# Bias attention, then a cosine-gated FFN: weight passes, bias load and k loads in other slots

## The chip, the cores and the metric

The kernel runs on one core of a Trainium2 chip. Its time is in microseconds (us) of device time, from one launch to its end; a figure for a kernel is the median of its runs.

## The reference

Attention over 4 batches and 8 heads, 576 positions, head size 64, with an additive bias that a small network computes from the distance of two positions, followed by a feed-forward layer with a cosine gate on the 2304 rows of 512:

```
scores = q @ k.T / 8 + bias[h]          # bias = relu((log1p(|i-j|) / log1p(max(i,1))) * w1 + b1) @ w2
x = softmax(scores) @ v                 # (4, 8, 576, 64), reshaped to (2304, 512)
h = x @ w_in                            # w_in (512, 2048)
out = (h * cos(h)) @ w_out              # w_out (2048, 512)
```

The weights arrive as 64-bit floats and are narrowed on the chip.

## The kernel before

The work is issued by hand, in program order, on every engine. There are three stages.

*Bias* (to about 67 us): TensorE, VectorE, ScalarE and GpSimd compute the bias of all heads, row group by row group, and SP stores each group to memory (`bias_store`, L335). Five query tiles share it: four of 128 queries and one of 64. `load_bias` (L233) reads the bias of a head pair and a tile back into SBUF, for the 64-query tile with two transfers of 64 rows each (L252).

*Attention* (to about 372 us): 16 units (`units`, L71), each a head pair and a batch. A unit has five query tiles; one tile is one *slot* (`slot(i)`, L541), so 80 slots, and slot i belongs to unit i // 5. The third slot of a unit is its tile 2, the fifth is the 64-query tile. In a slot TensorE issues the scores of the slot's tile (`qk`, L383, matmuls at L396, one set for each head, into two score banks `s` used in turn), and VectorE reads a set out with the bias added and the row extremum taken (L409; called the read-out here). ScalarE takes the exponent of the slot before (L427), VectorE its reciprocals (L439, L442), and GpSimd normalises it (L449). TensorE transposes the tile of three slots before (L456, L461); ScalarE and VectorE copy the result out (`keep_main`, `keep_both`, `keep_left`). TensorE multiplies the previous unit's transposed tiles by v (`pv`, L504) and turns the next unit's k and q (`turn`, L220, L195), which ScalarE copies out (L202 to L212). All transposes share three banks (`bank`, L182): each use takes the next in turn and waits for the copy that reads the fourth before it out. After a unit's k is turned, `kswap` (L214) moves its two halves to a second tile kS with two transfers (L216, L217); `qk` multiplies by kN and kS both.

In the same slots the first four chunks of the weights, eight *parts*, are loaded and narrowed into two operands: `load_w` (L76), an absolute value on ScalarE (`abs_w`, L89, L91), four passes of `widen_w` on VectorE (L99, L100, L102, L104; called the passes), a copy on ScalarE (L106) and a subtraction on GpSimd (L108). `W_PLAN` (L537) says in which of ten slots each step of a part stands, counted from slot 0, 10, 20 and so on. In a slot these steps are issued last, behind the copies. `LOAD_PLAN` (L536) says in which slot of a unit SP issues the loads: q of two units on (second slot), k of three units on (first slot), v of the next (fifth slot), four transfers each. GpSimd splits k and q in the slots of `POOL_PLAN` (L527).

SP issues all transfers in program order, and each issue may have to wait (for a buffer, for data, or for an earlier transfer); the ones behind it wait too.

*Feed-forward* (from about 372 us): `ffn1`, gate, `ffn2` in 96 steps, with the other 24 weight parts narrowed in three further groups of steps each (`begin_widen`, L727).

Of the kernel before, what the change touches and what calls it, by code (L numbers as in the profile page):

```python
# [23 lines left out]
def f(ap):  # L24
    return ap.bitcast(F32)
# [3 lines left out]
def kernel(  # L29
# [64 lines left out]
    def widen_w(fc, part, step=None):  # L94
        r, t, b = raw[fc, part], W[fc], wabs[fc, part]
        lo, hi = r[:, :, 0], r[:, :, 1]
        u = b.bitcast(U32)
        if step in (None, 0):
            nc.vector.tensor_scalar(b, b, 2.0**-15, None, ALU.max)  # L99
            nc.vector.tensor_scalar(u, u, 3, 0x3FFFFFF8, ALU.logical_shift_left, ALU.bitwise_and)  # L100
        if step in (None, 1):
            nc.vector.scalar_tensor_tensor(u, lo, 29, u, ALU.logical_shift_right, ALU.bitwise_or)  # L102
        if step in (None, 2):
            nc.vector.scalar_tensor_tensor(u, hi, 0xC0000000, u, ALU.bitwise_and, ALU.bitwise_or)  # L104
        if step in (None, 3):
            nc.scalar.activation(out=t[:, 0, part], in_=b, func=AF.Copy)  # L106
        if step in (None, 4):
            nc.gpsimd.tensor_tensor(t[:, 1, part], b, f(t[:, 0, part]), ALU.subtract)  # L108

    with tc.manual_schedule():  # L110
# [109 lines left out]
        def turn(u, ops):  # L220
            if u >= NU:
                return
            for op in ops:
                if op == "swap":
                    kswap(u)
                elif op[1] == "l":
                    tleft(u, op[0])
                else:
                    tmain(u, op[0], int(op[1]))
# [147 lines left out]
        def alloc_half(u, hf):  # L377
            PT[u, hf] = ptp.tile([128, 2, 4, WQ[hf]], F32, tag=f"h{hf}", name=f"PT{hf}")
            PX[u, hf] = px.tile([128, WQ[hf]], F32, tag=f"x{hf}", name=f"PX{hf}")
# [3 lines left out]
        def qk(u, j, h):  # L383
            t = tiles[j]
            s = ps_s.tile([128, 2, 512], F32, tag="s", name="s")
            if t < 4:
                o = 128 * t + 704 * h
                stats = [(qTs[u % 2][:, o : o + 128], h)]
            else:
                stats = [(qTs[u % 2][:, 512:640], 0), (qTs[u % 2][:, 576:704], 1)]  # L390
            for hf in range(2):
                n = 0
                for a, hh in stats:
                    c0 = HALF * hf + (640 if t == 4 else 576) * hh
                    for kt in (kN, kS):
                        nc.tensor.matmul(  # L396
                            s[:, hf, 0:HALF],
                            a,
                            kt[u][:, c0 : c0 + HALF],
                            start=(n == 0),  # L400
                            stop=(n == 2 * len(stats) - 1),
                        )
                        n += 1
            hp = units[u][0]
            if h == 0:
                P[u, j] = pp.tile([128, 1152], F32, tag="p", name="P")
            neg = P[u, j][:, 576 * h : 576 * h + 576]
            m = sv.tile([128, 2], F32, tag=f"m{h}", name="m")
            nc.vector.tensor_tensor_reduce(  # L409
                neg.rearrange("p (a x) -> p a x", a=2),  # L410
                s[:, :, 0:HALF],
                bias[hp, t, h].rearrange("p (a x) -> p a x", a=2),
                1.0,
                3.0e38,
                ALU.add,
                ALU.min,
                m[:, 0:1],
            )
            cur[u, j, h] = (neg, m)
# [3 lines left out]
        def softmax_exp(u, j, h):  # L423
            neg, m = cur.pop((u, j, h))
            if h == 0:
                dn[u, j] = sv.tile([128, 2], F32, tag="dn", name="dn")
            nc.scalar.activation(  # L427
                out=P[u, j][:, 576 * h : 576 * h + 576],
                in_=neg,
                func=AF.Exp,  # L430
                bias=m[:, 0:1],
                scale=-1.0,
                accum_out=dn[u, j][:, h : h + 1],
            )
# [16 lines left out]
        def ptrans(u, j, h):  # L451
            ps = bank()
            p = P[u, j]
            for c in range(4):
                o = 640 * h + 128 * c
                nc.tensor.transpose(ps[:, 128 * c : 128 * c + 128], p[:, o : o + 128], ident)  # L456
            return ps

        def ptrans_left(u, j):
            ps = bank()  # L460
            nc.tensor.transpose(ps[:, 0:128], P[u, j][:, 512:640], ident)  # L461
            return ps
# [11 lines left out]
        def keep_main(u, j, h, ps):  # L474
            hf, o = where(j)
            (act_copy if h == 0 else dve_copy)(
                PT[u, hf][:, h, :, o : o + 128], ps.rearrange("p (c x) -> p c x", c=4)
            )
# [54 lines left out]
        ]  # L533
        T_EARLY = [["k0", "k1"], ["kl", "swap"], ["q0"], ["ql"], ["q1"]]
        PV_EARLY = [[(-1, 0, (0, 1))], [(-1, 0, (2, 3, 4))], [], [(-1, 1, (0, 1))], [(-1, 1, (2, 3, 4))]]
        LOAD_PLAN = [[(3, "k")], [(2, "q")], [], [], [(1, "v")]]  # L536
        W_PLAN = [("load", 1), ("abs", 5), (0, 6), (1, 6), (2, 7), (3, 9), (4, 9)]  # L537
        get = lambda i: jobs[i] if 0 <= i < len(jobs) else None
        wparts = [(fc, p) for fc in range(WPRE) for p in range(2)]

        def slot(i):  # L541
            u, j = divmod(i, 5)
            now, last, prev = get(i), get(i - 1), get(i - 3)
            heads = lambda x: range(2 if tiles[x[1]] < 4 else 1)
            if now:
                qk(u, j, 0)
            if last:
                softmax_exp(*last, 0)
            if now and tiles[j] < 4:
                qk(u, j, 1)  # L550
            turn(u + 1, T_EARLY[j])
            if last and len(heads(last)) == 2:
                softmax_exp(*last, 1)
            for du, hf, chunks in PV_EARLY[j]:
                if 0 <= u + du < NU:
                    pv(u + du, hf, chunks)
            if i == 1:
                load_bias(0, tiles[-1])
            if prev:
                if prev[1] in (0, 2):  # L560
                    alloc_half(prev[0], prev[1] // 2)
                pt = [ptrans(*prev, h) for h in heads(prev)]
                pl = ptrans_left(*prev)
            if last:
                recip(*last, 0)
                recip(*last, 1)
            if prev:
                if len(pt) == 2:
                    keep_main(*prev, 0, pt[0])
                    keep_main(*prev, 1, pt[1])  # L570
                else:
                    keep_both(prev[0], pt[0])
            if last:
                for h in heads(last):
                    norm(*last, h)
            if prev:
                keep_left(*prev, pl)
            if now:
                for du, x, step in POOL_PLAN[j]:
                    if u + du < NU:  # L580
                        split(u + du, x, step)
                for du, x in LOAD_PLAN[j]:
                    if u + du < NU:
                        load(u + du, x)
                hp, b = units[u]
                if b == B - 1 and hp + 1 < HP:
                    load_bias(hp + 1, tiles[j])
                if u == NU - 1 and j < KD:
                    split_x(0, 0, j)
                for step, at in W_PLAN:  # L590
                    w, r = divmod(i - 0 - at, 10)
                    if r == 0 and 0 <= w < len(wparts):
                        if step == "load":
                            load_w(*wparts[w])
                        elif step == "abs":
                            abs_w(*wparts[w])
                        else:
                            widen_w(*wparts[w], step)
# [113 lines left out]
        loaded, widened, work = 0, 0, []  # L712
# [8 lines left out]
        def widen_step(p, ops):  # L721
            for step in ops:
                widen_w(*p, step)
            if 4 in ops:
                load_next()

        def begin_widen():  # L727
            nonlocal widened
            p = parts[widened]
            W[p[0]] = slots[p[0] % (2 * GF)]  # L730
            abs_w(*p)
            work.extend(lambda s=s: widen_step(p, s) for s in ((0,), (1,), (2, 3, 4)))
            widened += 1

        def ffn_step(i):
# [89 lines left out]
```

## Time and profile before

| | us |
|---|---|
| median of 3 runs (lowest, highest) | 791.92 (790.4, 793.26) |
| profiled execution, its own time | 787.1 |
| its span, first to last instruction | 785.3 |
| TensorE busy in the span | 742.6 |
| VectorE, ScalarE, GpSimd busy | 596.2, 471.2, 407.0 |
| mean granted TensorE clock (share of full) | 0.990 |

The rows further down come from this one execution. A time in front of an instruction is its start from the span's beginning; the second number is its length; in square brackets stand the idle time of its engine before it and what the profile takes for the releaser. PE is TensorE, PEld its weight load, DVE VectorE, ACT ScalarE, POOL GpSimd, SPq the queue in which SP issues transfers. L409 is line 409 of the kernel.

### The profile page before, as it was taken

How to read it: one execution, taken by the hardware profiler on the slowest of the kernel's cores; microseconds unless marked ns; L12 is line 12 of the kernel's file. 1: busy time of each engine (PE TensorE's matmuls, PEld its weight loads, DVE VectorE, ACT ScalarE, POOL GpSimd, SP SyncE). 2: the span in 40 equal slices, each digit the busy share in tenths (PEclk: the TensorE clock that was granted, in tenths of full speed). 3: DMA queues.
4: the chain of work that ended last, by engine and by line, in shares of the span. 5: the costliest groups of instructions: out<-in, count | busy, mean ns of one | idle time of the engine just before them, and what ended most of it. 6: DMA issues, size and time to landing. Idle time of an engine off the chain costs nothing.

```text
span 785.3 us, 13422 instructions
## 1 busy us (share of the span) xinstructions
PE 742.6 (95%) x4602; PEld 604.8 (77%) x4602; DVE 596.2 (76%) x1313; ACT 471.2 (60%) x991; POOL 407.0 (52%) x493
## 2 busy tenths in 40 slices
PE   6888799999999999999899999999999999999997
PEld 2216677777787777776789989988888888898996
DVE  8787477776767677776568878989899898976655
ACT  4997477777777777775355655544454545444332
POOL 2334366767676666658335536455445373544400
PEclk9999699999999999999999999999999999999999
DMA  4787535654673465330010101010111101001112
GB/s 130 237 298 211 128 79 128 173 122 105 133 193 86 119 171 134 70 95 28 1 54 28 54 28 55 27 54 28 54 38 43 54 28 54 1 23 46 53 42 81
DMA packets 70595, 68.45 MB, mean 87 GB/s; under 512 B 30080, under 2 KB 54784, under 8 KB 70528
## 3 DMA queue, kind: packets, MB, share of 16 engines
q1 hardware_dynamic: 70528, 67.60, 31.2%
q8 instruction: 37, 0.61, 0.3%
q14 instruction: 30, 0.25, 0.1%
HBM read 42.00 MB, written 15.61 MB: 73 GB/s over the span
## 4 chain that ended last, share of the span: by engine, by line
PE 83%; DVE 6%; ACT 4%; DMA 3%; issue 3%; POOL 1%; SPq 1%; ACTq 0%; DVEq 0%; POOLq 0%
PE ph L627 25%; PE po L682 24%; PE pv L513 11%; PE s L396 9%; PE pt L456 8%; PE pa L318 3%; PE pt L195 2%; DVE wb L100 1%; ACT rt L334 1%; DMA bt<-sc 1%; DVE P L409 1%; POOL ht L313 1%; PE pt L461 1%; DMA sc<-rt 1%; DVE PT L472 1%
## 5 line engine op out<-in xcount | busy, mean ns | idle before, releaser
L449 POOL TENSOR_SCALAR P<-P,rc 128x576 f32<-128x576 f32 x144 | 109.4, 771 | 90.4 <-DVE rc L442 65.9
L631 ACT ACTIVATE a<-ph,quarter 128x384 int32<-128x384 f32 x96 | 55.8, 581 | 108.0 <-PE ph L627 106.8
L427 ACT ACTIVATE P<-P,m 128x576 f32<-128x576 f32 x144 | 111.0, 771 | 8.6 <-DVE m L409 7.8
L409 DVE CUSTOM_DVE_ANT_0 P<-s,bt 128x576 f32<-128x576 f32 x144 | 103.6, 753 | 14.6 <-DMA vN<-in_v_dram 6.3
L396 PE MATMUL s<-kN,qT 128*128 128x288 f32 x320 | 96.5, 323 | 17.2 <-DVE m L409 17.1
L637 DVE SCALAR_TENSOR_TENSOR r<-a,ph 128x384 f32<-128x384 int32 x96 | 52.9, 551 | 77.9 <-ACT a L631 77.8
L499 POOL TENSOR_TENSOR xs<-xT,xs 128x384 fp32r<-128x384 f32 x96 | 107.2, 1116 | 8.0
L627 PE MATMUL ph<-xs,wpre 128*128 128x384 f32 x576 | 109.4, 338 | 0.8 <-DVE a L646 0.8
L627 PE MATMUL ph<-xs,w 128*128 128x384 f32 x576 | 108.3, 337 | 0.5 <-DVE a L646 0.5
L627 PEld LDWEIGHTS ph<-xs,wpre 128*128 128x128 f32 x576 | 101.8, 188 | 6.3 <-DVE a L646 2.1
L627 PEld LDWEIGHTS ph<-xs,w 128*128 128x128 f32 x576 | 101.3, 188 | 5.5 <-DVE a L646 1.4
L642 ACT ACTIVATE r<-r,hpi 128x384 f32<-128x384 f32 x96 | 59.3, 617 | 69.1 <-DVE r L638 69.1
L396 PE MATMUL s<-kS,qT 128*128 128x288 f32 x320 | 88.4, 297 | 0.1
L456 PEld LDWEIGHTS pt<-ident,P 128*128 128x128 f32 x576 | 63.4, 144 | 29.8 <-issue 8.4
L498 POOL TENSOR_SCALAR xs<-xT 128x384 fp32r<-128x384 f32 x96 | 61.4, 639 | 45.7 <-PE ph L627 45.7
L456 PE MATMUL pt<-ident,P 128*128 128x128 f32 x576 | 81.7, 284 | 2.2 <-POOL P L449 2.2
L472 DVE COPY PT<-pt 128x512 f32<-128x512 f32 x64 | 44.0, 687 | 50.5 <-PE pt L456 50.4
L513 PE MATMUL pv<-PT,vN 128*64 128x320 f32 (+1 forms) x512 | 77.4, 422 | 4.3 <-ACT PT L469 4.1
L396 PEld LDWEIGHTS s<-kN,qT 128*128 128x128 f32 x320 | 60.8, 190 | 21.4 <-DVE m L409 20.1
L682 PE MATMUL po<-w,gh 128*128 128x512 f32 x288 | 75.3, 396 | 0.0
L682 PE MATMUL po<-wpre,gh 128*128 128x512 f32 x288 | 75.2, 396 | 0.0
L656 DVE TENSOR_TENSOR gl<-a,gh 128x384 fp32r<-128x384 f32 x96 | 74.1, 772 | 0.6 <-ACT gh L650 0.6
(88 smaller groups left out, 1343.8 us busy)
## 6 DMA issues: line engine op xcount, KB each, us to landing
sc<-rt SPq DMA_DIRECT2D x36, 295.5 KB
kS<-kN SPq DMA_DIRECT2D x32, 304.0 KB
raw<-in_moe_w_in_dram SPq DMA_DIRECT2D x16, 512.0 KB
raw<-in_moe_w_out_dram SPq DMA_DIRECT2D x16, 512.0 KB
bt<-sc SPq DMA_DIRECT2D x16, 288.0 KB
nk<-in_k_dram SPq DMA_DIRECT2D x32, 128.0 KB
nq<-in_q_dram SPq DMA_DIRECT2D x32, 128.0 KB
vN<-in_v_dram SPq DMA_DIRECT2D x32, 128.0 KB
```

Source lines behind the costliest of these rows:

```text
L396: nc.tensor.matmul(s[:, hf, 0:HALF], a, kt[u][:, c0 : c0 + HALF], start=(n == 0), stop=(n == 2 * len(stats) - 1),)
L409: nc.vector.tensor_tensor_reduce(neg.rearrange("p (a x) -> p a x", a=2), s[:, :, 0:HALF], bias[hp, t, h].rearrange("p (a x) -> p a x", a=2 ...
L427: nc.scalar.activation(out=P[u, j][:, 576 * h : 576 * h + 576], in_=neg, func=AF.Exp, bias=m[:, 0:1], scale=-1.0, accum_out=dn[u, j][:, h ...
L449: nc.gpsimd.tensor_scalar(p, p, r, 1.0, ALU.mult, ALU.mult)
L456: nc.tensor.transpose(ps[:, 128 * c : 128 * c + 128], p[:, o : o + 128], ident)
L498: nc.gpsimd.tensor_scalar(h, src, 1.0, 1.0, ALU.mult, ALU.mult)
L499: nc.gpsimd.tensor_tensor(l, src, f(h), ALU.subtract)
L513: nc.tensor.matmul(ps[64 * h : 64 * h + 64, 0 : WQ[hf]], a, m, start=(c == 0), stop=(c == 4), tile_position=(0, 64 * h), skip_group_check= ...
L627: nc.tensor.matmul(ps, a, x, start=(i == 0), stop=(i == 3 * KD - 1))
L642: nc.scalar.activation(out=r, in_=r, func=AF.Sin, scale=SIN_SCALE, bias=hpi)
L656: nc.vector.tensor_tensor(gl, a, f(G[key][0]), ALU.subtract)
L682: nc.tensor.matmul(O[n][i], a[:, 128 * i : 128 * i + 128], w, start=(i0 == 0 and p == 0), stop=(i0 == GF - 1 and p == 2),)
```

## The change

The first of VectorE's two passes of step 0 keeps its number, the second becomes step 0.5. `W_PLAN` becomes a table by slot, with a table of its own for the first part (`W_FIRST`), and may reach into the ten slots before. Parts 1 to 7 get: load three slots before their ten, abs in their first slot, the passes L99, L100, L102 in the slots of index 2, 4 and 7, and L104 with the copy L106 and the subtraction L108 in index 9. Part 0 gets: load at 1, abs and L99 at 5, L100 and L102 at 6, L104 at 7, L106 and L108 at 9. The load of the 64-query tile's first bias moves from slot 1 to slot 0, and the k loads move from a unit's first slot to its third. The feed-forward stage's grouping is rewritten so that it stays as it was.

```diff
--- before.py
+++ after.py
@@ -97,6 +97,7 @@
         u = b.bitcast(U32)
         if step in (None, 0):
             nc.vector.tensor_scalar(b, b, 2.0**-15, None, ALU.max)
+        if step in (None, 0.5):
             nc.vector.tensor_scalar(u, u, 3, 0x3FFFFFF8, ALU.logical_shift_left, ALU.bitwise_and)
         if step in (None, 1):
             nc.vector.scalar_tensor_tensor(u, lo, 29, u, ALU.logical_shift_right, ALU.bitwise_or)
@@ -533,8 +534,9 @@
         ]
         T_EARLY = [["k0", "k1"], ["kl", "swap"], ["q0"], ["ql"], ["q1"]]
         PV_EARLY = [[(-1, 0, (0, 1))], [(-1, 0, (2, 3, 4))], [], [(-1, 1, (0, 1))], [(-1, 1, (2, 3, 4))]]
-        LOAD_PLAN = [[(3, "k")], [(2, "q")], [], [], [(1, "v")]]
-        W_PLAN = [("load", 1), ("abs", 5), (0, 6), (1, 6), (2, 7), (3, 9), (4, 9)]
+        LOAD_PLAN = [[], [(2, "q")], [(3, "k")], [], [(1, "v")]]
+        W_FIRST = {1: ["load"], 5: ["abs", 0], 6: [0.5, 1], 7: [2], 9: [3, 4]}
+        W_PLAN = {-3: ["load"], 0: ["abs"], 2: [0], 4: [0.5], 7: [1], 9: [2, 3, 4]}
         get = lambda i: jobs[i] if 0 <= i < len(jobs) else None
         wparts = [(fc, p) for fc in range(WPRE) for p in range(2)]
 
@@ -554,7 +556,7 @@
             for du, hf, chunks in PV_EARLY[j]:
                 if 0 <= u + du < NU:
                     pv(u + du, hf, chunks)
-            if i == 1:
+            if i == 0:
                 load_bias(0, tiles[-1])
             if prev:
                 if prev[1] in (0, 2):
@@ -587,9 +589,9 @@
                     load_bias(hp + 1, tiles[j])
                 if u == NU - 1 and j < KD:
                     split_x(0, 0, j)
-                for step, at in W_PLAN:
-                    w, r = divmod(i - 0 - at, 10)
-                    if r == 0 and 0 <= w < len(wparts):
+                for w, at in ((i // 10, i % 10), (i // 10 + 1, i % 10 - 10)):
+                    plan = W_PLAN if w else W_FIRST
+                    for step in plan.get(at, []) if w < len(wparts) else []:
                         if step == "load":
                             load_w(*wparts[w])
                         elif step == "abs":
@@ -729,7 +731,7 @@
             p = parts[widened]
             W[p[0]] = slots[p[0] % (2 * GF)]
             abs_w(*p)
-            work.extend(lambda s=s: widen_step(p, s) for s in ((0,), (1,), (2, 3, 4)))
+            work.extend(lambda s=s: widen_step(p, s) for s in ((0, 0.5), (1,), (2, 3, 4)))
             widened += 1
 
         def ffn_step(i):
```

## Rows read from the trace of the kernel before

**Rows 1.** Busy time by stretch; columns: stretch, its length, then the engines named, clock, DMA.

```profile
60.00:90.00 30.00, 23.45 (x158) 17.40 (x155) 16.19 (x45) 17.10 (x39) 11.77 (x18) 0.79 0.67 180
...
160.00:195.00 35.00, 33.27 (x270) 26.99 (x270) 25.74 (x77) 27.03 (x66) 23.69 (x32) 1.00 0.46 115
```

**Rows 2.** Waits from 88 to 372 us; total, times, longest.

```profile
PE s L396 <- DVE m L409: 12.9, 8, 2.4
```

**Rows 3.** VectorE's instructions: read-outs that begin slots 20, 25 and 30 (start, us, what).

```profile
144.11 0.75 DVE L409 CUSTOM_DVE_ANT_0 P<-s,bt 128x576 f32<-128x576 f32 x1
...
161.68 0.75 DVE L409 CUSTOM_DVE_ANT_0 P<-s,bt 128x576 f32<-128x576 f32 x1
...
180.82 0.75 DVE L409 CUSTOM_DVE_ANT_0 P<-s,bt 128x576 f32<-128x576 f32 x1
```

**Rows 4.** All engines' instructions around the gap of slots 16 to 18.

```profile
132.52 0.42 DVE L99 TENSOR_SCALAR wb<-wb 128x512 f32<-128x512 f32 x1
...
134.40 0.75 DVE L409 CUSTOM_DVE_ANT_0 P<-s,bt 128x576 f32<-128x576 f32 x1
...
135.21 0.40 PE L396 MATMUL s<-kN,qT 128*128 128x288 f32 x1 [1.49 <-DVE m L409]
...
136.28 1.90 POOL L449 TENSOR_SCALAR P<-P,rc 128x576 f32<-128x576 f32 x2 [2.81 <-DVE rc L442]
...
136.50 1.07 DVE L104 SCALAR_TENSOR_TENSOR wb<-raw,wb 128x512 uint32<-128x512 uint32 x1
```

**Rows 5.** All engines' instructions at the start, slots 4 and 5.

```profile
80.44 0.58 PE L396 MATMUL s<-kS,qT 128*128 128x288 f32 x1
...
84.28 0.76 DVE L409 CUSTOM_DVE_ANT_0 P<-s,bt 128x576 f32<-128x576 f32 x1 [6.25 <-DMA vN<-in_v_dram]
...
85.10 0.61 PE L396 MATMUL s<-kN,qT 128*128 128x288 f32 x1 [3.61 <-DVE m L409]
```

**Rows 6.** SP's own waits from 60 to 110 us; total, times, longest.

```profile
SPq L153 <- DMA bt<-sc: 2.6, 1, 2.6
...
SPq L148 <- DMA kS<-kN: 0.7, 1, 0.7
...
SPq L157 <- DMA nk<-in_k_dram: 0.5, 2, 0.3
```

**Rows 7.** SP's issues from 71 us (start, length of the merged issues, what).

```profile
73.11 3.29 SPq L252 DMA_DIRECT2D bt<-sc  x2
...
76.75 1.00 SPq L157 DMA_DIRECT2D nq<-in_q_dram  x2
...
80.32 1.25 SPq L148 DMA_DIRECT2D vN<-in_v_dram  x2
...
84.14 1.11 SPq L153 DMA_DIRECT2D vN<-in_v_dram  x2
```

**Rows 8.** All engines, 154 to 165 us: behind a third slot, then a fifth.

```profile
154.50 0.76 DVE L409 CUSTOM_DVE_ANT_0 P<-s,bt 128x576 f32<-128x576 f32 x1
...
156.44 0.38 PE L396 MATMUL s<-kN,qT 128*128 128x288 f32 x1
...
164.54 0.38 PE L396 MATMUL s<-kN,qT 128*128 128x288 f32 x1
```

**Rows 9.** Instructions on tile wb; times are ns, shortest/median/longest.

```profile
L99 DVE TENSOR_SCALAR wb<-wb x32: 416/727/1234, 95.8 to 680.5; 128x512 f32<-128x512 f32 x32
...
L102 DVE SCALAR_TENSOR_TENSOR wb<-raw,wb x32: 677/688/1506, 97.1 to 684.9; 128x512 uint32<-128x512 uint32 x32
```

**Rows 10.** All engines, end of slot 19 and slot 20.

```profile
143.36 0.63 ACT L106 ACTIVATE wpre<-wb 128x512 fp32r<-128x512 f32 x1
...
143.88 0.77 ACT L427 ACTIVATE P<-P,m 128x576 f32<-128x576 f32 x1
...
144.77 1.17 ACT L202 ACTIVATE kN<-pt 128x512 fp32r<-128x512 f32 x2
...
146.02 1.09 PE L456 MATMUL pt<-ident,P 128*128 128x128 f32 x8
```

## The prediction

> **What bounds the kernel now.** I read the busy time by stage first, then the waits, then the instructions around each wait. In the attention stage TensorE is busy 33.27 of 35.00 us at a granted clock of 1.00 [rows 1]: there, time is won only where TensorE stands still or where its clock falls. The waits of that stage name one thing beside the start: score matmuls (L396) waiting for the DVE read-out at L409, 12.9 us in eight gaps, the longest 2.4 [rows 2]. A slot is one query tile, and ten slots carry one weight part. The halves of such ten differ: from slot 20's first read-out to slot 25's it is 161.68 - 144.11 = 17.57 us, and from there to slot 30's 19.14 [rows 3]. The second half carries the gap, 1.49 us at 135.21 in slots 6 to 8 of its ten, and [rows 4] show its maker. Three weight passes stand on VectorE from 132.52 to 134.40, 1.88 us in one piece, and the read-out that frees the score bank stands behind them, at 134.40. So a gap is paid once per part, and the clean half is the measure of what remains.
>
> The start is a second stage, with a granted clock of 0.79 from 60 to 90 us [rows 1]. There the read-out of the 64-query tile begins at 84.28 after 6.25 us idle, and TensorE stands 3.61 us until 85.10 [rows 5]. The profile names a v transfer as releaser, but the read-out reads no v. SP's own waits tell more: the issue at 84.14 had waited 2.6 us for a bias transfer [rows 6, 7]. So the second half of the tile's bias, whose issue ended at 73.11 + 3.29 = 76.40, landed at about 84.1.
>
> **The passes, part by part.** For parts 1 to 7 the first two passes move into the third and fifth slots, the next into the eighth (a third slot of its unit), the last into the tenth (a fifth slot); part 0 keeps its old slots except that the first pass goes one slot earlier. No pass is added or dropped.
>
> *Removed:* the gap. Six whole parts at 19.14 - 17.57 = 1.57 give 9.4 us. Part 0 still has two of three passes in its seventh slot, so I take half a gap, 0.7 (ends 0.4 and 1.5). In the last part the gap is the longest, 2.4, but GpSimd there also splits x for the next stage and takes up some of it: 1.6 (ends 0.7 and 2.4). Sum 11.7.
>
> *Third slot:* the read-out behind a moved pass ends at 154.50 + 0.76 = 155.26, and the matmul that needs its bank begins at 156.44 [rows 8]: 1.18 us of cover. A pass stood in such a slot already: L104 at 136.50 took 1.07 beside GpSimd's normalising [rows 4], and no gap follows it in [rows 2]. Price 0. Without that cover it would cost its own length.
>
> *Fifth slot:* cover 164.54 - (161.68 + 0.75) = 2.1 us [rows 3, 8]; the longest of any such pass is 1.51 [rows 9]. Price 0.
>
> The measured row speaks for small stretching: 1.07 is 0.39 over the shortest 0.68 of its kind (L102's, [rows 9]). [...]
>
> *Added:* the last pass now stands in the same slot as the ScalarE copy (L106) that reads it. Before, that copy ran at 143.36 without waiting [rows 10]. The new pass can begin only after the slot's copies, where the read-out stands now, 144.11 [rows 3], and at 0.69 ends at 144.80. The copy starts at about 144.86, 1.5 us late, and queued behind it on ScalarE are the exp (143.88) and the two k copies (144.77, 1.17 for two) [rows 10]. Those keep their distances of 0.52 and 0.89: the first k copy begins at 146.27 and ends near 146.9. A TensorE transpose of that slot needs the bank which it frees (three banks in turn, the fourth user waits for the first). The second group of four of the eight transposes from 146.02 would start at 146.02 + 1.09/2, about 146.5 [rows 10]. It waits about 0.45, and the next one for the second k copy 0.1: 0.55 us. The nearest rows bound it between 0 and 1.5 (the whole lateness). I take 0.55, near the lower end, because the rows give each step of it. ScalarE's next part begins there too, its abs moving from the sixth slot of its ten to the first; it stands behind the k copies and meets idle time within two slots. Six times (slots 20 to 70; after the last part no k is left to turn): 3.3 us given back. GpSimd's subtraction moves with the copy, some 1.5 us later, and its normalising behind it is needed only three slots on: 0.
>
> *Weight loads* move to three slots before their abs instead of four, about 10.6 us; the longest landing that the start shows is 84.1 - 75.8 = 8.3. Price 0. The feed-forward stage keeps its passes grouped as they are: 0.
>
> **The start.** The bias of the 64-query tile goes ahead of the k swap; the four k transfers (288 KB) go from before the swap to two slots later. The bias must wait until its tile's last store has landed, which was so by 73.11, where it is issued now [rows 7]; a wait up to then costs nothing, since the bias before it lands only near 75.8. On SP the swap, q and the weight load are queued behind it. In the kernel before transfers landed in the order of their issue: the first k piece by 76.75 (SP waited for it), the second swap piece at 80.32 (0.7 waited), the bias at 84.14 [rows 6, 7]. TensorE read the swapped k at 80.44, right behind its landing [rows 5]: that transfer has no slack. In the new order the swap loses the k pieces ahead of it (about 1.5 us: from 75.8, where the bias before them had landed and SP's second issue of the pair began, to the second piece) and gets the bias ahead (84.1 - 80.3 = 3.8): it lands at 80.3 - 1.5 + 3.8 = 82.6. So the wait for the bias goes, and the swap is late next. The second head's matmuls, 85.10 before, follow 1.0 behind the landing, at 83.6: gain 1.5. The ends: +4.7 if the swap is not late (3.6 of gap, and some 1.1 of work at the lower clock), -0.5 if both bias halves take 2.9, as the second did after the first (84.1 less 81.2, where the second of the two v issues at 80.32 ended its wait; the swap then lands at 84.6). I take 1.5, which the order of landing gives. [...] Later k loads have four slots, some 14 us, instead of six until GpSimd splits them: 0.
>
> **Sum.** 11.7 + 1.5 - 3.3 = 9.9 us. The profiled execution took 787.1 us (785.3 of span): 777.2 by it. It lies 4.8 below the median of the runs shown, 791.92; from that median the prediction is **782.0**.
>
> **Rivals.**
> 1. *The swap is not late.* A later transfer finishes before an earlier one. For it: the new order issues no later than before; against it: the landings in order [rows 6, 7]. 3.2 more gain: 778.8. [...]
> 2. *ScalarE's lateness does not reach TensorE.* The 0.55 rests on which bank is free; idle time on ScalarE speaks for it, the bank order against. 3.3 more: 778.7.
> [...]
> 4. *Slower: the late copy on ScalarE becomes the new stall.* Place: exp and k copies behind L106 in each tenth slot. It decides from (11.7 + 1.5)/6 = 2.2 us per part on. If the last pass, held by GpSimd, took the longest of its kind, 1.51 [rows 9], the copy would come 2.3 late; with the abs queued on top (about 0.6, as long as the copy, [rows 10]) and all of it passed to TensorE it is 2.9, and 6 x 2.9 = 17.4 against 13.2: 796.1. Against it: the bank wait ends with the first k copy.
>
> **Numbers.** Forecast 0.52, rivals in order 0.17, 0.15, 0.12, 0.04. The forecast's own bounds run from 778 to 787; the first two rivals together give 775.5. The range is 775.5 to 787.5. A measurement of this kernel tells 0.3% (2.4 us) from no change: faster 0.92; within it 0.05 (the lower ends of the start, part 0 and the last part together); slower 0.03.
>
> **What would show it.** Right: no L396 gap in slots 17, 27 and so on; halves of about 17.6 and 18.1 us; a wait of L106 for L104 of 0.6 to 1.5 in the tenth slots and a transpose (L456) gap of about half a us behind it; at the start, swapped k as the last thing that TensorE waits for. Wrong: L409 still following a pass with TensorE idle, gaps of over 2 us at the transposes, or k splits and abs waiting for their loads.

## The result, and the profile after

| | before | after |
|---|---|---|
| median of the runs shown, us (lowest, highest) | 791.64 (790.4, 793.26) | 782.77 (781.15, 784.3) |
| profiled execution, its own time; its span | 787.1; 785.3 | 783.67; 781.6 |
| mean granted TensorE clock | 0.990 | 0.988 |

The ratio is 0.9892, with an interval of 0.9862 to 0.9922: 1.1% faster. The forecast of 782.0 us was met within a us; of its steps, two were off by 2 to 4 us, in opposite directions. Line numbers after the first pass are one or two higher than before: the score matmul is L397 (was L396), the read-out L410 (L409), the passes L99, L101, L103, L105, the copy L107 (L106), GpSimd's subtraction L109, the transposes L457 and L462.

**The stage.** The busy time by stretch, of the kernel after (stretch, its length, PE, PEld, DVE, ACT, POOL, clock, DMA share, GB/s), as [rows 1] show it of before, with one stretch more:

```profile
60.00:90.00 30.00, 23.42 (x167) 17.05 (x160) 17.39 (x47) 18.39 (x42) 12.45 (x18) 0.83 0.69 181
160.00:195.00 35.00, 34.41 (x277) 27.21 (x276) 25.52 (x80) 27.44 (x69) 24.01 (x33) 1.00 0.44 107
290.00:300.00 10.00, 7.72 (x51) 6.45 (x49) 4.77 (x16) 7.22 (x20) 4.48 (x7) 0.83 0.78 180
```

From 160 to 195 us TensorE is now busy 34.41 of 35.00 us, where it was 33.27 [rows 1]. The third line is new: ten us in which the clock falls in the middle of the stage; the kernel before had TensorE busy for all of these ten us, at a clock of 1.00. The waits from 88 to 372 us (total, times, longest), beside [rows 2]:

```profile
ACT wpre L107 <- DVE wb L105: 8.2, 6, 1.4
ACT wb L91 <- DMA raw<-in_moe_w_in_dram: 7.4, 3, 4.0
...
PE pt L462 <- ACT kN L213: 2.3, 1, 2.3
...
PE s L397 <- DVE m L410: 1.0, 1, 1.0
```

The last line is what was the first: 12.9 us in eight gaps are 1.0 in one, part 0's. The first line is the copy that now follows its pass directly, as the prediction had it (1.4 us, six times). The second was not foreseen: ScalarE's absolute value waits three times for the weights to land.

**Ten slots.** VectorE's instructions that begin slots 30, 35 and 40 of the kernel after, to be held against [rows 3]:

```profile
178.24 0.75 DVE L410 CUSTOM_DVE_ANT_0 P<-s,bt 128x576 f32<-128x576 f32 x1
...
195.94 0.75 DVE L410 CUSTOM_DVE_ANT_0 P<-s,bt 128x576 f32<-128x576 f32 x1
...
213.78 0.75 DVE L410 CUSTOM_DVE_ANT_0 P<-s,bt 128x576 f32<-128x576 f32 x1
```

The halves are 17.70 and 17.84 us, where they were 17.57 and 19.14: the gap has gone, and the halves are nearly alike. The passes in the new slots, from the view of tile wb from 90 to 372 us (ns, shortest/median/longest):

```profile
L99 DVE TENSOR_SCALAR wb<-wb x8: 417/804/832, 91.7 to 334.9; 128x512 f32<-128x512 f32 x8
L101 DVE TENSOR_SCALAR wb<-wb x8: 417/417/417, 95.4 to 342.1; 128x512 uint32<-128x512 uint32 x8
L103 DVE SCALAR_TENSOR_TENSOR wb<-raw,wb x8: 1034/1063/1098, 95.8 to 351.1; 128x512 uint32<-128x512 uint32 x8
```

Beside GpSimd L99 takes 0.80 us instead of 0.42, and L103 1.06, where L105, of the same kind, takes 0.68. Neither reaches the longest of [rows 9], and no L397 waits behind them. GpSimd stretches too, as VectorE's and GpSimd's instructions from 184 to 190 us and from 205 to 208 us show: its normalising of two heads, 1.47 us where no pass meets it, takes 1.63 beside L99 and 1.90 beside L103.

```profile
184.23 1.47 POOL L450 TENSOR_SCALAR P<-P,rc 128x576 f32<-128x576 f32 x2 [0.45 <-ACT xT L470]
...
188.21 1.63 POOL L450 TENSOR_SCALAR P<-P,rc 128x576 f32<-128x576 f32 x2 [1.88 <-ACT PT L470]
188.43 0.80 DVE L99 TENSOR_SCALAR wb<-wb 128x512 f32<-128x512 f32 x1
...
205.78 1.90 POOL L450 TENSOR_SCALAR P<-P,rc 128x576 f32<-128x576 f32 x2 [1.96 <-ACT PT L470]
206.00 1.07 DVE L103 SCALAR_TENSOR_TENSOR wb<-raw,wb 128x512 uint32<-128x512 uint32 x1
```

The lengths of ten slots, each the difference of two such starts (first read-out of slot 0, 10, 20 and so on to 70; the last column goes from slot 70 to 79), put all kernels of this study side by side. The labels are explained with the experiments.

| | 0 | 10 | 20 | 30 | 40 | 50 | 60 | 70 to 79 |
|---|---|---|---|---|---|---|---|---|
| before, of the rows ahead | 40.56 | 36.68 | 36.71 | 36.64 | 36.68 | 36.71 | 36.64 | 33.16 |
| before, profiled again (e8) | 40.64 | 36.67 | 36.68 | 36.71 | 36.66 | 36.65 | 36.68 | 34.32 |
| after | 38.64 | 35.72 | **36.04** | 35.54 | **36.22** | 35.54 | **39.16** | 30.63 |
| after, profiled again (e9) | 38.60 | 35.73 | **36.43** | 35.53 | **37.59** | 35.49 | **36.33** | 30.63 |
| after, old start (e1) | 39.89 | 35.70 | **39.07** | 35.52 | **37.68** | 35.51 | **37.19** | 30.61 |
| before, new start (e2) | 38.81 | 36.64 | 37.71 | 36.70 | 37.35 | 38.30 | 36.67 | 34.31 |
| weight loads earlier (e3) | 37.78 | 35.67 | 35.53 | 35.52 | 35.54 | 35.54 | 35.49 | 30.62 |
| old pass slots (e4) | 37.52 | 36.66 | 36.67 | 36.67 | 36.67 | 36.68 | 36.74 | 33.18 |
| e3, swap first (e5) | 39.54 | 35.73 | 35.52 | 35.50 | 35.53 | 35.52 | 35.50 | 30.63 |
| e3, copy later too (e7) | 38.67 | 35.72 | 35.14 | 35.10 | 35.11 | 35.09 | 35.48 | 30.24 |
| e3, bias as rows (e6) | 30.37 | 35.72 | 35.50 | 35.53 | 35.48 | 35.50 | 35.55 | 30.58 |
| after, bias as rows (e10) | 30.37 | 35.67 | 35.49 | 35.55 | 35.55 | 35.54 | 35.51 | 30.63 |
| before, bias as rows (e11) | 31.79 | 36.66 | 36.70 | 36.69 | 36.71 | 36.65 | 36.72 | 33.19 |
| e7, bias as rows, part 0 spread (e12) | 29.89 | 35.14 | 35.13 | 35.12 | 35.13 | 35.11 | 35.13 | 30.21 |

In bold are the tens that begin with a late weight load. The largest of them, seen in the instructions of all engines from 284 to 297 us of the kernel after:

```profile
284.68 0.37 SPq L79 DMA_DIRECT2D raw<-in_moe_w_in_dram  x1
...
292.57 0.66 ACT L91 ACTIVATE wb<-raw 128x512 f32<-128x512 f32 x1 [4.03 <-DMA raw<-in_moe_w_in_dram]
...
294.32 0.33 PE L462 MATMUL pt<-ident,P 128*128 128x128 f32 x1 [2.28 <-ACT kN L213]
...
295.07 0.45 PE L397 MATMUL s<-kN,qT 128*128 128x288 f32 x1
```

The load of part 6, planned for slot 57, is issued at 284.68, 0.9 us before the read-out of slot 60 (285.54), and lands at 292.57, 7.9 us later. ScalarE stands for it 4.03 us with the copies of k queued behind, the transposes of TensorE stand 2.28 for those copies, and the matmuls that follow run at a lower clock (0.50 from 295 to 297 us): 0.45 us for a matmul of 128x288 at 295.07, where one at 294.75 had taken 0.30. Slot 61 took 7.00 us so; slot 31, in a ten without a late load, took 3.76.

In the kernel before, the read-out of slot 57 began at 281.14, and SP was then busy with reloads of the bias for the next heads, as its issues from 250 us show:

```profile
281.35 7.43 SPq L239 DMA_DIRECT2D bt<-sc  x9
```

**The start**, all engines from 78 to 92 us of the kernel after, beside [rows 5]:

```profile
81.20 0.76 DVE L410 CUSTOM_DVE_ANT_0 P<-s,bt 128x576 f32<-128x576 f32 x1 [1.83 <-DMA bt<-sc]
...
84.54 0.58 PE L397 MATMUL s<-kS,qT 128*128 128x288 f32 x1 [3.37 <-DMA nk<-in_k_dram]
...
90.69 0.38 PE L397 MATMUL s<-kN,qT 128*128 128x288 f32 x1
```

and SP's issues in the same kernel, from 70 us, in place of [rows 7]:

```profile
70.62 1.08 SPq L253 DMA_DIRECT2D bt<-sc  x2
71.75 0.53 SPq L217 DMA_DIRECT2D kS<-kN  x1
...
79.46 0.37 SPq L79 DMA_DIRECT2D raw<-in_moe_w_in_dram  x1
...
81.06 1.72 SPq L158 DMA_DIRECT2D nk<-in_k_dram  x2
...
84.42 1.11 SPq L163 DMA_DIRECT2D nk<-in_k_dram  x2
```

The read-out of the 64-query tile begins at 81.20 instead of 84.28, and now TensorE stands 3.37 us before the matmul with kS. The releaser that the line names is a k load of the input; the matmul reads kS. SP's own waits from 60 to 110 us, beside [rows 6], tell more:

```profile
SPq L163 <- DMA kS<-kN: 1.6, 1, 1.6
```

The issue at 84.42 had waited for the swap, which so landed at about 84.4. The swap is late next, as forecast.

**The lateness of the copy**, all engines from 176 to 182 us (slots 29 and 30) of the kernel after, where [rows 10] show slot 20 of before:

```profile
177.64 0.68 DVE L105 SCALAR_TENSOR_TENSOR wb<-raw,wb 128x512 uint32<-128x512 uint32 x1
178.35 0.63 ACT L107 ACTIVATE wpre<-wb 128x512 fp32r<-128x512 f32 x1 [1.36 <-DVE wb L105]
...
179.53 1.44 PE L457 MATMUL pt<-ident,P 128*128 128x128 f32 x8
...
179.65 1.13 ACT L203 ACTIVATE kN<-pt 128x512 fp32r<-128x512 f32 x2
180.32 0.42 PEld L457 LDWEIGHTS pt<-ident,P 128*128 128x128 f32 x4 [0.36 <-ACT kN L203]
```

The eight transposes take 1.44 us instead of 1.09 [rows 10]: a stop of 0.35 in their middle, where the second four wait for the first k copy to free their bank (with three banks, a use waits for the copy that reads the third use before it). The step is the predicted one.

### The profile page after: what moved, and what is told of

Same layout as the page of the kernel before. It is cut to its first block, busy times and chain, and to the rows that moved or that the text cites. A ratio compares the mean times of both kernels' runs of the same rounds, so it can differ in the third digit from the quotient of the medians.

```text
span 781.6 us, 13415 instructions
## 1 busy us (share of the span) xinstructions
PE 745.4 (95%) x4602; PEld 605.4 (77%) x4602; DVE 593.2 (76%) x1313; ACT 467.8 (60%) x991; POOL 407.5 (52%) x493
## 4 chain that ended last, share of the span: by engine, by line
PE 79%; DMA 9%; ACT 6%; DVE 3%; issue 1%; SPq 1%; POOL 0%; ACTq 0%; DVEq 0%
PE ph L629 25%; PE po L684 24%; PE pv L514 9%; PE s L397 8%; PE pt L457 7%; PE pa L319 3%; DMA raw<-in_moe_w_in_dram 3%; DMA bt<-sc 2%; PE pt L196 2%; ACT P L428 2%; DMA sc<-rt 2%; DMA kS<-kN 1%; ACT rt L335 1%; PE pt L462 1%; ACT PT L470 1%
## 5 line engine op out<-in xcount | busy, mean ns | idle before, releaser
L450 POOL TENSOR_SCALAR P<-P,rc 128x576 f32<-128x576 f32 x144 | 110.9, 782 | 74.2 <-DVE rc L443 45.0
L410 DVE CUSTOM_DVE_ANT_0 P<-s,bt 128x576 f32<-128x576 f32 x144 | 103.8, 753 | 12.2 <-PE s L397 5.0
L397 PE MATMUL s<-kN,qT 128*128 128x288 f32 x320 | 96.8, 324 | 1.7 <-DVE m L410 1.6
L397 PE MATMUL s<-kS,qT 128*128 128x288 f32 x320 | 89.0, 299 | 3.4 <-DMA nk<-in_k_dram 3.4
L457 PEld LDWEIGHTS pt<-ident,P 128*128 128x128 f32 x576 | 62.7, 143 | 32.3 <-issue 11.2
L457 PE MATMUL pt<-ident,P 128*128 128x128 f32 x576 | 82.4, 283 | 3.3 <-POOL P L450 2.5
L109 POOL TENSOR_TENSOR w<-wb,w 128x512 fp32r<-128x512 f32 x16 | 20.7, 1297 | 90.0 <-ACT w L107 90.0
```

The lines of the kernel that those rows point to most:

```text
L397: nc.tensor.matmul(s[:, hf, 0:HALF], a, kt[u][:, c0 : c0 + HALF], start=(n == 0), stop=(n == 2 * len(stats) - 1),)
L410: nc.vector.tensor_tensor_reduce(neg.rearrange("p (a x) -> p a x", a=2), s[:, :, 0:HALF], bias[hp, t, h].rearrange("p (a x) -> p a x", a=2 ...
L450: nc.gpsimd.tensor_scalar(p, p, r, 1.0, ALU.mult, ALU.mult)
```

## The experiments

Theory T: the passes take the gaps away, the late copy gives a part of it back, the swap bounds the start, and late weight loads cost what the tens in bold show. Its rivals are those of the prediction, and that the start's order or the reload of the bias itself matters more than T says. Ratios are against the kernel before on the same chip.

**Where the start's time comes from.** e1 is the kernel after with the old start; e2 is the kernel before with the new start alone.

```diff
 # e1, in the kernel after; e2 makes the opposite edit in the kernel before
-        LOAD_PLAN = [[], [(2, "q")], [(3, "k")], [], [(1, "v")]]
+        LOAD_PLAN = [[(3, "k")], [(2, "q")], [], [], [(1, "v")]]
...
-            if i == 0:
+            if i == 1:
                 load_bias(0, tiles[-1])
```

> The changed kernel, with the bias of the 64-query tile and the k loads back where they stood before. Theory (the swap of k is late next, so the start is worth about 1.5 us): 784.3 us, 1.5 above the changed kernel's 782.8; at the start the read-out waits some 6 us again and TensorE 3.6. Rival (the start was worth 4.7): 787.5.

> The kernel before with the start's part of the change alone. Theory: 1.5 us under before, 790.1 us, and TensorE waits for the swapped k, landing near 84 us, instead of for the read-out; the eight gaps of 1.5 us stay. Rival (the start was worth 4.7): 786.9.

e1 took 786.62 us, ratio 0.9948 [0.9923, 0.9974]; e2 788.08, ratio 0.9964 [0.9942, 0.9986]. The first line is of the instructions of e1 near 86 us, the second fence of those of e2 near 83 us:

```profile
86.04 0.61 PE L397 MATMUL s<-kN,qT 128*128 128x288 f32 x1 [3.64 <-DVE m L410]
```

```profile
83.43 0.58 PE L396 MATMUL s<-kS,qT 128*128 128x288 f32 x1 [2.85 <-DMA nk<-in_k_dram]
```

With the old start TensorE stands 3.64 us for the read-out, that is, for the bias; with the new one alone, 2.85 for the swap: one wait in place of the other. The first ten slots go from 39.89 (e1) to 38.64 (after), and from 40.6 (before) to 38.81 (e2): 1.3 and 1.8 us. The times do not hit the expectation: 786.62 is 3.9 above the kernel after, 788.08 is 2.7 below its own before, where theory T had 1.5 and the rival 4.7. In e1 a part of this lies behind the start: it lost more to weight loads (9.6 us of waits of L91, against 7.4), and its slots 10 to 79 are 2.4 us longer. In e2 three tens (from slots 20, 40 and 50) are 0.6 to 1.6 us longer than those of before, though no abs waits for a load there; in the first two TensorE waits for a late swap, 1.2 us in all. So in this execution the new order of the loads has a price behind the start as well, which the prediction put at 0. Its time was 792.07, 4.0 above the median of e2, so how much of this a usual run has stays open.

**The weight loads.** e3 issues each load four slots earlier and leaves all else of the change.

```diff
-        W_PLAN = {-3: ["load"], 0: ["abs"], 2: [0], 4: [0.5], 7: [1], 9: [2, 3, 4]}
+        W_PLAN = {-7: ["load"], 0: ["abs"], 2: [0], 4: [0.5], 7: [1], 9: [2, 3, 4]}
```

> The changed kernel with the weight parts' loads issued seven slots before their abs instead of three, so ahead of the bias reloads of slots 15 to 19, 35 to 39 and 55 to 59. Theory (parts 2, 4 and 6 come late behind those reloads: abs waited 1.6 to 4.0 us, and the tens from slot 20, 40 and 60 took 36.04, 36.22 and 39.16 us against 35.54): those tens fall to about 35.55 us, 4.8 us in all, to 778.0 us, and abs waits for no load. Rival (ScalarE has idle time for such waits, the long tens have another cause): abs no longer waits but the tens keep their lengths, 782 to 783 us.

777.02 us, ratio 0.9824 [0.9792, 0.9856]. No wait of L91 for raw is left, and all tens from slot 20 to 70 are 35.5 us. Against the kernel after, the three tens give 36.04 + 36.22 + 39.16 - 3 x 35.54 = 4.8 us in the first profile and 3.8 in the second, and the medians 5.8. The load of part 6 in e3, among SP's issues from 256 us:

```profile
258.52 1.31 SPq L79 DMA_DIRECT2D raw<-in_moe_w_in_dram  x1
```

That is 23.8 us before the read-out of slot 60 in that kernel (282.36). The first ten slots are 0.9 shorter than in the kernel after as well; e7, with the same start, has them 38.67, so that part is no more than the start's own spread.

**The passes.** e4 has the new start and the loads three slots ahead of their ten, but abs and the passes of parts 1 to 7 in their old slots.

```diff
-        W_PLAN = {-3: ["load"], 0: ["abs"], 2: [0], 4: [0.5], 7: [1], 9: [2, 3, 4]}
+        W_PLAN = {-3: ["load"], 5: ["abs"], 6: [0, 0.5, 1], 7: [2], 9: [3, 4]}
```

> The changed kernel with abs and the four passes of parts 1 to 7 back in their old slots (indices 5, 6, 6, 6, 7, 9), its loads and start kept. Theory (the gain is the gap behind three passes): the gaps of about 1.5 us return in seven slots, 11.0 us, while the copy's lateness (0.4 us in each of six tens) and the waits for loads (4.8 us) go: 786.6 us. Rival (the gain came from the loads and the start): no dearer than the changed kernel, 778 to 783 us.

787.45 us, ratio 0.9959 [0.9935, 0.9983], 10.4 above e3. The wait of before is back, as its waits from 88 to 372 us show:

```profile
PE s L397 <- DVE m L410: 12.4, 8, 2.4
```

The tens are 36.67 again, 1.14 above e3's 35.53, and the last stretch 33.18 against 30.62. By these lengths the passes are worth 6 x 1.14 + 2.56 = 9.4 us, with the price of the late copy already taken off.

**The copy.** e7 adds to e3 that the copy and the subtraction of parts 1 to 6 go two slots later (the loop looks one part further back, and the last part keeps its slots).

```diff
+        W_LAST = {-7: ["load"], 0: ["abs"], 2: [0], 4: [0.5], 7: [1], 9: [2, 3, 4]}
-        W_PLAN = {-7: ["load"], 0: ["abs"], 2: [0], 4: [0.5], 7: [1], 9: [2, 3, 4]}
+        W_PLAN = {-7: ["load"], 0: ["abs"], 2: [0], 4: [0.5], 7: [1], 9: [2], 11: [3, 4]}
```

> The kernel of e3 with the copy L107 and the subtraction L109 of parts 1 to 6 two slots after the last pass (index 11) instead of in its slot. Theory (the copy's wait of 1.36 us for the pass delays the k copies and so a transpose, 0.4 us in each of six tens): L107 no longer waits, the tens fall from 35.53 to about 35.15 us, 2.4 us in all, to 774.6. Rival (the wait lies in idle time, the tens are long for another reason): the tens keep 35.5 us and the time stays at 776.5 to 777.5.

776.13 us, ratio 0.9824 [0.9796, 0.9851]. ScalarE and TensorE at slots 29 and 30 of e7:

```profile
176.16 1.17 ACT L203 ACTIVATE kN<-pt 128x512 fp32r<-128x512 f32 x2 [0.55 <-PE pt L196]
...
177.41 1.09 PE L457 MATMUL pt<-ident,P 128*128 128x128 f32 x8
```

The k copies no longer stand behind the weight copy, and the transposes take 1.09 again. Tens of 35.53 become 35.11 in four places and the last stretch falls from 30.62 to 30.24, so the lateness cost about 0.4 each. The ten from slot 60 stayed at 35.48: slots 63 to 65 were 0.4 longer, for a reason that stays open. The time fell by only 0.9, where 2.4 had been expected. In the profiled execution the first ten came out 0.9 longer than in e3; whether it did so in the other runs, no profile tells. The tens are the sounder measure here, and e12 below repeats them.

**The order at the start.** e5 is e3 with the bias of the 64-query tile behind the swap again, k still two slots later.

```diff
-            if i == 0:
+            if i == 1:
                 load_bias(0, tiles[-1])
```

> The kernel of e3 (777.0 us) with the bias of the 64-query tile issued behind the swap of k again, the k loads staying two slots later. Theory (transfers land in the order of their issue, so one of the two is always late): the swap lands near 79 us and the matmuls on kS do not wait; the tile's bias lands near 82.6 and the read-out waits again; TensorE stands about as long, the time is within 1.5 us of e3, 775.5 to 778.5. Rival (only the swap's place matters): 3 us or more under e3, 774 us or less.

778.58 us, ratio 0.9851 [0.9824, 0.9879]. All engines near 86 us:

```profile
85.31 0.76 DVE L410 CUSTOM_DVE_ANT_0 P<-s,bt 128x576 f32<-128x576 f32 x1 [5.83 <-DMA bt<-sc]
...
86.13 0.61 PE L397 MATMUL s<-kN,qT 128*128 128x288 f32 x1 [3.58 <-DVE m L410]
```

TensorE waits for the bias as before, though the k loads are out of the way: moving k alone does nothing for it. Whichever of bias and swap goes second is late. The order is worth 1.6 in the medians, 0.9 to 1.8 in the first ten (39.54, against 38.67 in e7 and 37.78 in e3).

**The form of the reload.** So both are slow to land. In e6 (on e3) the bias is stored with other strides, so that the reload of a tile is one pattern of 128 rows (64 for the last tile), instead of 8 (or 4) groups of 16 rows. Bytes, issues and order stay.

```diff
+    RS = 608
+    GS = 128 * RS - 16
...
-                                [[128 * RB, 8], [8 * RB - 1, 16], [1, n]],
+                                [[8 * RS - 1, 128], [1, n]],
...
-                            [[128 * RB, 4], [8 * RB - 1, 16], [1, S]],
+                            [[8 * RS - 1, 64], [1, S]],
```

> The kernel of e3 with the bias stored so that a reload is one pattern of 128 rows (64 for the 64-query tile) in place of 8 or 4 groups of 16; bytes and order of the issues stay. Theory (the reloads land late because of the form of their pattern, not their bytes alone): the tile's bias and the swap land some 2 to 4 us sooner at the start, TensorE's wait for kS shrinks from 5.0 us to under 2, the time falls by 2 to 4 us, to 773 to 775. Rival (bytes alone set the landing): the wait stays near 5 us, 776.5 to 777.5.

769.07 us, ratio 0.9724 [0.9697, 0.9752]: 8.0 below e3, where 2 to 4 had been expected. Busy time from 60 to 90 us in e3, then in e6, and last, from the view of tile bt in e6 from 60 to 372 us, what its loads took to land:

```profile
60.00:90.00 30.00, 22.55 (x172) 17.46 (x168) 17.32 (x48) 18.46 (x42) 12.62 (x18) 0.89 0.70 187
```

```profile
60.00:90.00 30.00, 27.66 (x217) 21.15 (x213) 24.66 (x66) 24.84 (x60) 16.18 (x23) 1.00 0.79 223
```

```profile
DMA to landing us min/median/max: 2.6/3.3/4.3
```

The reloads land in 3.3 us, the longest in 4.3; before, one had taken 84.1 - 76.4 = 7.7. No wait for bias or swap is left, the granted clock from 60 to 90 us is 1.00 instead of 0.89, and the first ten slots take 30.37 us instead of 37.78. The comparison goes as far as the one landing of the old form goes: 7.7 us with 4 groups of 16 rows, 4.3 at most with one pattern of 128 or 64. Why the new form lands sooner, no view here shows. The step from row to row in memory changed with the pattern (from 592 to 608 elements), and no run separates the two.

**Does the reload also make the weight loads late?** e10 is the kernel after with e6's reload, loads still three slots ahead; e11 is the kernel before with that reload alone.

> The changed kernel with the bias stored so that a reload is one pattern of 128 (or 64) rows, as in e6; the weight loads stay three slots before their abs. Theory (the weight loads of parts 2, 4 and 6 come late because the reloads ahead of them land slowly in their old form): abs waits for no load, the tens are 35.5 us, the start as in e6 (first ten 30.4 us), 769 to 770 us. Rival (the bytes of the reloads are enough to make the loads late): abs still waits some 5 us and the time is 774 us or more.

> The kernel before with only the form of the bias reload changed as in e6. Theory (the start's wait comes from that form; the order of the transfers there then matters little): the first ten falls from 40.6 to 31 to 33 us, the eight gaps of 1.5 us stay, 781 to 783 us. Rival (the order of the issues is needed too): the read-out or kS still keeps TensorE waiting for more than 2 us at the start, 785 us or more.

e10 took 768.51 us, ratio 0.9715 [0.9678, 0.9752], as long as e6 within their spread; e11 780.2, ratio 0.9865 [0.9827, 0.9903]. The waits from 88 to 372 us of e10, then the same of e11 (with this edit abs is L93, and the score matmul of e11 is L400):

```profile
ACT wb L93 <- DMA raw<-in_moe_w_in_dram: 1.1, 2, 1.0
```

```profile
PE s L400 <- DVE m L413: 12.9, 8, 2.4
```

With the quicker reload the waits for weights fall from 7.4 to 1.1 without any load moved, and their tens are 35.5. In e10 the load of part 6 goes out at 272.22, 10.5 us after the swap's second piece in SP's order (261.69); in the kernel after that stretch is 284.68 - 272.63 = 12.1, and the load then takes 7.9 to land, where e10's longest took 6.4. So both SP's queue behind the reloads and the landing itself made the loads late. e11 keeps its eight gaps: the passes' gain stands apart from all this, and is larger in this company: the change is worth 791.64 - 782.77 = 8.9 us with the old reload, and 780.2 - 768.51 = 11.7 with the new one.

**The profiles themselves.** e8 is the kernel before and e9 the kernel after, unchanged, each profiled once more.

> The kernel before, unchanged, for a second profile of it. Theory (its runs spread because transfers at the start and behind the bias reloads land sooner or later from run to run): the gaps of 1.49 us stand in the same eight places, and the first ten slots or the tens from slot 20, 40 or 60 differ by some us from the first profile. Rival (the difference lies elsewhere): the slots agree to 0.3 us and the feed-forward stage differs.

> The changed kernel, unchanged, for a second profile beside the runs of this call. Theory (its time spreads with the landing of the weight loads of parts 2, 4 and 6): 781 to 785 us; abs waits again for three loads, 5 to 10 us in all, and the tens from slots 20, 40 and 60 are long by other amounts than in the first profile, the others 35.5 us. Rival (the three long tens were chance): no such wait, tens of 35.5 us, about 778 us.

e8 took 790.88 us (span 789.0), e9 783.13, ratio 0.9908 [0.9879, 0.9937] (span 780.2). The loads come late in e9 again, at the same three places but by other amounts:

```profile
ACT wb L91 <- DMA raw<-in_moe_w_in_dram: 6.9, 3, 2.9
```

The table shows that the first seven tens of before repeat to 0.1 us, so the expectation of e8 failed: neither the start nor the reloads set its two profiles apart. What set the first one 3.7 us under e8 is elsewhere: 0.5 ahead of slot 0 (66.87 against 67.37), 1.1 in slot 78 (3.09 against 4.21), and 2.0 behind slot 79's read-out (785.3 - 360.65 = 424.65, against 789.0 - 362.38 = 426.62). Why these differ between executions stays open.

**All together.** e12 joins early loads, later copy and the row reload, and spreads part 0's passes too.

```diff
-        W_FIRST = {1: ["load"], 5: ["abs", 0], 6: [0.5, 1], 7: [2], 9: [3, 4]}
+        W_FIRST = {1: ["load"], 5: ["abs", 0], 6: [0.5], 7: [1], 9: [2], 11: [3, 4]}
```

> The changed kernel with all that helped: weight loads seven slots before abs, the reload in one pattern of rows, copy and subtraction two slots behind the last pass, and part 0's passes one to a slot (indices 5, 6, 7, 9, copy at 11). Theory (the parts add up): from e6's 769.1 the copy's lateness goes (2.4 us) and the first part's gap of 1.1 us, 765.6 us. Rival (the copy's place is hidden elsewhere, as e7's time alone suggests): 767.5 us or more.

765.0 us, ratio 0.9676 [0.9642, 0.9711], the fastest here, 17.8 below the kernel after. From 88 us on no wait of the score matmul (L401 here) for the read-out is left, in part 0 either, and the tens are 35.13. From e6 to e12 the medians fall by 4.1, of which the table shows 3.4: 2.5 in the six tens (the copy), 0.5 in the first (part 0) and 0.4 in the last stretch.

## Why the prediction was right, and where it was wrong

The two profiles e8 and e9 lie 8.8 us of span apart, and the table gives that by stretch. Beside it stands the prediction's sum:

| step | forecast | from the table (e9 - e8) |
|---|---|---|
| start (slots 3 to 5) and part 0 (slot 6) | -1.5 - 0.7 = -2.2 | -1.2 - 0.8 = -2.0 |
| six tens: gaps away, copy late | -9.4 + 3.3 = -6.1 | 6 x (35.53 - 36.67) = -6.8 |
| weight loads | 0 | +3.9, the rest of the six tens (0.2 of it in the ten from slot 10, which has no late load) |
| last stretch | -1.6 | 30.63 - 34.32 = -3.7 |
| before slot 0, and behind | 0 | -0.1 |
| sum | -9.9 | -8.8 |

- **The gaps.** Right in place and size. A ten lost 36.67 - 35.13 = 1.54 in e12, where the copy is out of the way; 1.57 had been read from the halves. In e4 the gaps come back with nothing but the passes.
- **Third and fifth slots at price 0.** Right: in the third slots L99 took 0.80 and L103 1.06, under the cover of 1.18; in the fifth L101 took 0.42 and L105 0.68 (but for the last part), under 2.1; and no gap follows. The chance of 0.12, third of the rivals', stood for a price of these slots from the longest passes of the whole kernel, 1.23 and 1.51 [rows 9]; none came near them here. Where the two meet, a pass begins 0.22 behind the start of GpSimd's first normalising (188.43 against 188.21) and takes some 0.39 more than alone: L99 0.80 instead of 0.42, L103 1.07, where L105 alone took 0.68. GpSimd's pair, 1.47 alone, takes 1.63 beside L99 and 1.90 beside L103. What sets these amounts, no view here shows.
- **The copy's lateness.** Right by mechanism, a little too dear: 0.42 each (e7), or 2.5 in all (e6 to e12), instead of 0.55 and 3.3. Of the two small waits in the sum only the first was seen, 1.44 - 1.09 = 0.35 at the transposes. Rival 2, that it costs nothing, falls.
- **The start.** Right: the bias's wait goes, the swap's takes its place. Worth 0.9 to 1.8 in the first ten over the pairs of kernels above, 1.5 forecast; the medians of e1 and e2 give 3.9 and 2.7, which hold what the order of the loads does behind the start too. The swap landed at 84.4 in a run whose slot 0 began at 67.84, so at 83.4 on the scale of the first profile of before (66.87): between the 82.6 of the sum and its bound of 84.6. Rival 1 falls.
- **The step that failed: "Weight loads move to three slots before their abs instead of four, about 10.6 us; the longest landing that the start shows is 84.1 - 75.8 = 8.3. Price 0."** The 10.6 us were counted between slots. A load leaves when SP comes to it, and SP, in order, still had swap, q, k and bias reloads of the unit's first slots ahead: part 6's left 0.9 us before slot 60's read-out, not 10 before. The landing of 7.9 lay within the bound. Rows of before could have told it: the nine reloads of the bias that SP issues there from slot 57 on, shown with the ten slots above. It cost 3.8 to 4.8 us in the tens, and 5.8 in the medians with what e3 gained at the start. This is the path of rival 4 (ScalarE late in a ten's first slots, k copies behind it, TensorE's transposes standing), with another thing at its head; "What would show it" named both, abs waiting for a load and a gap of over 2 us at the transposes, as signs of being wrong, and both came; the sum had neither.
- **The last part** was taken too low: 2.6 (e4 to e3), not 1.6. GpSimd's work did not take up what had been left for it. The rest of the 3.7 is slot 78, which was 1.1 longer in e8 and in e2 than in the first profile of before, for a reason that stays open.
- **Why the total fits.** By luck: a cost of about 4 left out, against 2.1 too little for the last stretch (1.1 of it that slot 78) and 0.7 too little for the tens. To go from the median and not from the profiled execution was right: what set the first profile of before 3.7 us under e8 had nothing to do with the steps of the sum.

## What to carry to other kernels

Count the lead of a load from the issue that the trace shows, not from the slot that the plan gives it: SP issued part 6's load, planned for slot 57, behind everything that waited ahead of it, 0.9 us before the read-out of slot 60, and the load moved closer to its use inherited that. Single passes spread over slots with cover of their own (at most 1.10 us under 1.18) cost nothing here, while three passes in one piece of 1.88 us held the read-out. When swapping two transfers only swaps which of them is late, look at how long each takes to land: the pattern of the reload was worth 8 us here, its order 1 to 2.

## What the hardware showed that had not been expected

The reloads of the bias, the same bytes in the same number of issues, landed in 3.3 us in the median and in 4.3 at most as 128 or 64 rows (e6); the one landing that the waits of the kernel before give, as groups of 16 rows, took 7.7. The new form took away the waits at the start, raised the clock there (from 0.89 to 1.00) and ended most of the lateness of the weight loads (7.4 us of waits to 1.1). VectorE's pass and GpSimd's normalising, when they met, were longer than alone by 0.39 and 0.43 us (L103 beside the pair of L450), alike in parts 1 to 6. The clock: after the wait of 2.28 us at 294.32 the matmuls took 0.45 us instead of 0.30, at a granted clock of 0.50 from 295 to 297 us, and the ten us around it had 0.83; the 1.49 us gaps of the kernel before [rows 4] stood in a stage with a clock of 1.00 [rows 1].
